# Windowed attention and a convolutional gated feed-forward: the order of TensorE, VectorE, ScalarE and GpSimd written in the source, with the weights' rescale moved to ScalarE

## The chip, the cores and the metric

The kernel runs on one core of one Trainium2 chip, all of it in float32. The metric is the device time of one launch in microseconds (us). The engines are TensorE (PE; its weight loads are PEld), VectorE (DVE), ScalarE (ACT), GpSimd (POOL) and SyncE (SP), which issues the DMA transfers.

## The reference

There are 8 batches of 576 tokens, 8 heads of 64, a window of 128 tokens, a model width of 512 and 1024 hidden channels. The weights are given in float64.

```
scores = q @ k^T / 8 + slope[h] * -|i - j|       # slope[h] = 2^-(h+1)
scores = where(0 <= i - j < 128, scores, -1e9)
attn   = exp(scores - rowmax);  attn /= rowsum + 1e-9
x      = (attn @ v)  as [B, S, H*D]              # 8 x 576 x 512
h      = relu(x @ w_in)                          # 512 -> 1024
conv   = sum over k of conv_w[k] * h[token + k - 1]   # 3 taps per channel, zero outside the batch
out    = (h * sigmoid(conv)) @ w_out             # 1024 -> 512
```

## The kernel before

**Tiles.** The 4608 tokens make 36 tiles of 128. A batch is 4.5 tiles long, so that some tiles begin a batch, some hold a border in their middle, and some follow such a tile. A query tile needs its own keys and those of the tile before; because the window is exactly 128, each place of a 128 x 128 score block is taken by one of the two, and VectorE merges them: a masked copy (`COPY_PREDICATED`, L261) puts the earlier tile's scores over the masked half, and a tile at a batch border has a second masked copy, with a large constant (its row ends in `_SCALAR`). The heads go in two halves, u = 0 and 1, of four.

**One tile through the kernel.** Names in brackets are those of the profile's rows.

- `qkT` transposes q and k on TensorE (pt) and ScalarE copies them out (L234, qkT_all).
- `scores`: matmuls (L254, sc); two merges, each a masked copy (L261) and the addition of the bias (L276, which writes e); the row maximum (L277, st); four exponentials on ScalarE, one for each head (L279); then sum, reciprocal and product on VectorE (L287 to L289), the normalisation.
- `attnT`: transposes on TensorE (pa), a copy by ScalarE (L299, rl), and one or two triangular masks on GpSimd (L302, L305), which part the merged block into the two key tiles.
- `av`: the context matmuls (L323, av). The context x is kept as a high part in the reduced type fp32r (L331, ScalarE) and a low part, the rest (L332, VectorE). `xfin` copies a halo column to the neighbouring chunk (L346, L348).
- The feed-forward works in 18 chunks of two tiles, with a halo column at either side, and in four steps a chunk, each over 256 of the 1024 channels: 72 steps. An **up** step has 24 matmuls (L368, p), three for each product, high by high, high by low, low by high. For either half: relu (L373, hh), the middle tap as a copy with a scale (L374, z), and two filter operations for the outer taps on VectorE (L381). A batch border within the chunk cuts these in pieces: four rows where two stand otherwise. Then tanh (L387), the gate's product (L388), and the split into high and low part (L393 on ScalarE, L394 on GpSimd; gh and gl). A **down** step multiplies that by the second weight (L409, o); after a chunk's last down step ScalarE copies the result out (L415, ob) and SyncE stores it.

**Weights.** They come as pairs of 32-bit words, in 17 blocks: four of the first weight, the small one of the convolution, four more of the first weight, eight of the second. A staging tile (wst, three buffers) takes each block. GpSimd clamps the high word read as a float (L133) and multiplies it by 2^-112 (L134, to wg); VectorE shifts the low word (L135) and joins the bits in two operations (L136, L139); ScalarE casts to the high part (L177); TensorE subtracts the two (L191, L192, pw), and ScalarE casts the rest to the low part (L193). A block's staging tile becomes free after L139, and the load of a later block goes into it.

**What sets the order.** `manual_schedule` holds TensorE alone to the order of the source. The other engines' lists are made by a scheduler, which runs a model of the timeline and weighs priorities that the source gives (150 for the context, 100 for the transposes, 60 for the scores, 15 for loads, 0 or -15 for the rest of the up steps, 600 for their matmuls). From tile 5 on the source's order is one loop, a period:

```
SC(t, 0); SC(t, 1); AV(t - 1); DOWN(); UP(); QK(t + 1)
TR(t, 0); UP(); TR(t, 1); DOWN()
```

Here `SC` is scores, `TR` is attnT and `AV` is av with xfin. Each period holds two up and two down steps. In odd t the first up step begins a new chunk, and its matmuls read a column that comes from the tile of this period's `AV(t - 1)`. In even t it begins a chunk's second half, whose x is long there. Ahead of the loop `opening` holds tiles 0 to 4, with the calls `WT(start, finish)` in between, which convert 14 of the 17 weight blocks; the other three stand in period 5. All transposes, scores, up steps and weights share six PSUM buffers (`pst`, tag "tr").

Of the kernel before, what the change touches and what calls it, by code (L numbers as in the profile page):

```python
# [21 lines left out]
def tile_alibi_window_attention_conv_glu(  # L22
# [102 lines left out]

    def to_f32(st, g):

        lo, hi = st[..., 0], st[..., 1]
# [1 line left out]
        nc.gpsimd.tensor_scalar(out=hf, in0=hf, scalar1=HIMAX, scalar2=-HIMAX, op0=ALU.min, op1=ALU.max)  # L133
        nc.gpsimd.tensor_scalar(out=gf, in0=hf, scalar1=2.0**-112, scalar2=None, op0=ALU.mult)  # L134
# [33 lines left out]
    started = []  # L168

    def convert_weight():  # L170
        block, st = fetched.pop(0)
        g = wpool.tile([P, WB], U32, name="wg", tag="wg")
        if block is None:
            f = to_f32(st, g[: 3 * NFC, :P])
        else:
# [1 line left out]
            nc.scalar.copy(out=block[1][0], in_=f)  # L177
# [49 lines left out]
    def qkT(t, u):  # L227
# [6 lines left out]
        nc.scalar.copy(out=qkT_all[:, t % SLOTS, u], in_=ps)  # L234

    def scores(t, u):
        first = (t * P) % S
        slot = t % SLOTS
# [16 lines left out]
        for a in range(2):  # L255
            ps = pss[a]
            s_cur, s_prev = ps[:, :, cur, :], ps[:, :, prev, :]
            shp = [P, 2, P]

            def put(mask, data):  # L260
                nc.vector.copy_predicated(  # L261
                    out=s_cur, mask=mask.unsqueeze(1).to_broadcast(shp), data=data
                )
# [329 lines left out]
```

## Time and profile before

| | |
|---|---|
| launches, median of 3 | 715.4 us (714.04 to 716.02) |
| the profiled execution | 713.98 us, of it 712.3 us in the span |
| TensorE busy, matmul | 656.5 us, 92% of the span, 4881 matmuls |
| TensorE busy, weight load (beside matmuls) | 561.7 us, 79% |
| VectorE busy | 516.9 us, 73% |
| ScalarE busy | 448.1 us, 63% |
| GpSimd busy | 236.2 us, 33% |
| mean granted TensorE clock | 0.973 of full speed |

The times in a row are in us from the start of the span, unless a column says ns. A row of the stretches by engine has: the stretch and its length; then busy time and count of PE, PEld, DVE, ACT and POOL; the granted clock; the share of the DMA engines; GB/s. A row of the waits has: the waiting instruction, what released it; the sum in us, how many times, and the longest or typical of one. A row of the timeline has: the start, the duration, engine, line, operation, output and inputs, shape, count, and in brackets the idle time of the engine ahead of it and what ended it. A row of the groups has: line, engine, operation, shape, count; busy us and mean ns; idle time ahead and its releasers.

### The profile page before, as it was taken

To read this page: it belongs to the slowest core of one execution; us is meant where nothing else is said; L and a number is where in the kernel's file an instruction comes from. 1 tells how busy PE (TensorE), PEld (TensorE's weight loads), DVE (VectorE), ACT (ScalarE), POOL (GpSimd) and SP (SyncE) were. 2 spreads that over 40 slices of the span, in tenths; PEclk is the share of its full clock that TensorE was granted. 3 is DMA by queue.
4 is the path that set the end of the run, shared out by engine and by line. 5 is a ranking of instruction groups with operands and counts; after the bars stand their busy time and mean duration, and the time that the engine had idled before them with its cause. 6 is when DMAs were issued, how large, how long until landed. Compare 5 with 4: busy or idle time off the path is not lost.

```text
span 712.3 us, 13254 instructions
## 1 busy us (share of the span) xinstructions
PE 656.5 (92%) x4881; PEld 561.7 (79%) x4881; DVE 516.9 (73%) x1208; ACT 448.1 (63%) x1257; POOL 236.2 (33%) x251
## 2 busy tenths in 40 slices
PE   5766897999999989999999998999999989999997
PEld 3445675888888878887978887888888878887996
DVE  7865997768776877777677677768776877777452
ACT  4544665767676746675767675767676746675563
POOL 3443861232223223333323333332223323333321
PEclk9967999999999999999999999999999999999999
DMA  9642440222221312222312222222222312200000
GB/s 229 149 129 58 124 128 16 75 45 75 61 60 45 80 40 75 45 75 45 90 31 75 45 75 45 76 46 75 60 60 46 81 38 75 46 31 1 31 31 30
DMA packets 120101, 47.02 MB, mean 66 GB/s; under 512 B 113356, under 2 KB 113380, under 8 KB 120036
## 3 DMA queue, kind: packets, MB, share of 16 engines
q1 hardware_dynamic: 120036, 46.17, 25.5%
q8 instruction: 39, 0.64, 0.4%
q14 instruction: 26, 0.21, 0.1%
HBM read 36.72 MB, written 9.44 MB: 65 GB/s over the span
## 4 chain that ended last, share of the span: by engine, by line
PE 63%; DVE 23%; ACT 8%; DMA 4%; issue 2%; POOL 1%; SPq 0%; ACTq 0%; POOLq 0%; DVEq 0%
PE p L368 29%; PE o L409 16%; DVE z L381 5%; PE sc L254 5%; PE av L323 4%; DVE sc L261 4%; PE pt L233 4%; DVE e L276 3%; PE pa L296 3%; DVE st L277 3%; DMA wst<-in_moe_w_out_dram 2%; ACT e L279 2%; DVE z L388 2%; ACT z L387 1%; DVE e L289 1%
## 5 line engine op out<-in xcount | busy, mean ns | idle before, releaser
L381 DVE SCALAR_TENSOR_TENSOR z<-hh,cw,z 128x256 f32<-128x256 f32 (+7 forms) x384 | 177.2, 493 | 104.9 <-ACT z L374 101.4
L368 PE MATMUL p<-x,wi 128*128 128x258 f32 x1728 | 228.5, 289 | 22.7 <-ACT e L279 8.8
L368 PEld LDWEIGHTS p<-x,wi 128*128 128x128 f32 x1728 | 219.2, 194 | 31.9 <-ACT e L279 14.9
L409 PE MATMUL o<-wo,gh 128*128 128x512 f32 x576 | 187.0, 405 | 0.7 <-ACT wo L193 0.7
L279 ACT ACTIVATE e<-e,st 128x128 f32<-128x128 f32 x288 | 112.2, 391 | 64.2 <-DVE st L277 63.8
L394 POOL TENSOR_TENSOR gl<-z,gh 128x512 fp32r<-128x512 f32 x72 | 94.6, 1314 | 132.8 <-ACT gh L393 124.5
L302 POOL TENSOR_SCALAR_AFFINE_SELECT rl<-rl 128x512 f32<-128x512 f32 x64 | 46.2, 721 | 266.1 <-ACT rl L299 266.1
L409 PEld LDWEIGHTS o<-wo,gh 128*128 128x128 f32 x576 | 103.0, 188 | 26.6 <-issue 5.8
L409 PE MATMUL o<-wo,gl 128*128 128x512 f32 x288 | 113.9, 396 | 0.0
L373 ACT ACTIVATE hh<-p 128x258 f32<-128x258 f32 x144 | 55.0, 382 | 70.5 <-PE p L368 68.6
L388 DVE SCALAR_TENSOR_TENSOR z<-z,hh 128x512 f32<-128x512 f32 x72 | 51.1, 709 | 52.7 <-ACT z L387 52.6
L323 PE MATMUL av<-rl,rv 128*64 128x128 f32 x1088 | 70.6, 282 | 13.0 <-POOL rl L305 13.0
L323 PEld LDWEIGHTS av<-rl,rv 128*64 128x64 f32 x1088 | 60.2, 140 | 25.9 <-POOL rl L305 15.0
L387 ACT ACTIVATE z<-z 128x512 f32<-128x512 f32 x72 | 45.3, 630 | 51.4 <-DVE z L381 49.5
L374 ACT ACTIVATE z<-hh,cw 128x256 f32<-128x256 f32 x144 | 73.8, 512 | 5.8 <-ACT hh L373 0.4
L254 PE MATMUL sc<-qkT_all 64*128 64x256 f32 x512 | 69.2, 410 | 6.0 <-ACT qkT_all L234 5.2
L254 PEld LDWEIGHTS sc<-qkT_all 64*128 64x128 f32 x512 | 49.0, 196 | 24.2 <-issue 10.9
L305 POOL TENSOR_SCALAR_AFFINE_SELECT rl<-rl 128x512 f32<-128x512 f32 x72 | 57.0, 792 | 30.0 <-ACT rl L299 26.0
L409 PEld LDWEIGHTS o<-wo,gl 128*128 128x128 f32 x288 | 54.1, 188 | 12.9
L393 ACT CAST gh<-z 128x512 fp32r<-128x512 f32 x72 | 44.4, 616 | 25.3 <-DVE z L388 25.2
L276 DVE SCALAR_TENSOR_TENSOR e<-sc,bias 128x256 f32<-128x256 f32 x144 | 54.3, 415 | 0.0
L279 ACT ACTIVATION_READ_ACCUMULATOR e<-e,st 128x1 f32 x288 | 53.9, 187 | 0.0
(64 smaller groups left out, 662.5 us busy)
## 6 DMA issues: line engine op xcount, KB each, us to landing
out_dram<-ob SPq DMA_DIRECT2D x36, 256.0 KB, 2.0
rqk<-in_q_dram SPq DMA_DIRECT2D x32, 256.0 KB, 3.1
rqk<-in_k_dram SPq DMA_DIRECT2D x32, 256.0 KB, 3.7
rv<-in_v_dram SPq DMA_DIRECT2D x32, 256.0 KB, 2.8
wst<-in_moe_w_in_dram SPq DMA_DIRECT2D x8, 512.0 KB, 4.7
wst<-in_moe_w_out_dram SPq DMA_DIRECT2D x8, 512.0 KB, 3.5
rqk<-in_q_dram SPq DMA_DIRECT2D x8, 128.0 KB, 2.8
rqk<-in_k_dram SPq DMA_DIRECT2D x8, 128.0 KB, 3.1
```

The source lines that it names most:

```text
L254: nc.tensor.matmul(pss[a][:, g], qt, qkT_all[rows, win, u, 1, g, :], start=True, stop=True)
L276: nc.vector.scalar_tensor_tensor(out=heads, in0=s_cur, scalar=-0.125, in1=b, op0=ALU.mult, op1=ALU.add)
L279: nc.scalar.activation(out=e[:, j, :], in_=e[:, j, :], func=AF.Exp, bias=st[:, 0, j : j + 1], scale=-1.0, accum_out=st[:, 1, j : j + 1],)
L305: nc.gpsimd.affine_select(out=r, in_=r, pattern=[[0, HU], [1, P]], compare_op=ALU.is_ge, fill=0.0, base=0, channel_multiplier=-1)
L323: nc.tensor.matmul(ps[a * D : (a + 1) * D, u * NG + g], vraw[tt][:, u * HU + j], rl[:, side, j], start=n == 0, stop=n == len(sides) - 1,)
L368: nc.tensor.matmul(ps[:, :XW], a[:, cc, f * P : (f + 1) * P], x[:, cc, :], start=n == 0, stop=n == last)
L373: nc.scalar.activation(out=hh[:, ff, :], in_=ps[:, :XW], func=AF.Relu, scale=0.5)
L374: nc.scalar.activation(out=z[:, ff, :], in_=hh[:, ff, 1 : 1 + CW], func=AF.Copy, scale=cw[:, 1, f : f + 1])
L381: nc.vector.scalar_tensor_tensor(out=z[:, ff, a:cut], in0=hh[:, ff, a + kk : cut + kk], scalar=cw[:, kk, f : f + 1], in1=z[:, ff, a:cut], ...
L388: nc.vector.scalar_tensor_tensor(out=z, in0=z, scalar=1.0, in1=hh[:, :, 1 : 1 + CW], op0=ALU.add, op1=ALU.mult)
L394: nc.gpsimd.tensor_tensor(out=gl, in0=z, in1=as32(gh), op=ALU.subtract)
L409: nc.tensor.matmul(oo[m], g[:, ff, ms], w[:, f, :], start=f == 0 and n == 0, stop=f == NFC - 1 and n == 2)
```

## The change

**One list an engine.** `manual_schedule` now holds TensorE, VectorE, ScalarE and GpSimd to the order of the source; SyncE alone is left to the scheduler, and the priorities are gone. For this, functions are cut into pieces that can be placed singly: `scores` into `scores` (matmuls), `merge` (one masked copy and its addition; L283, L296), `rowmax` (L300), `exps` (L305) and `normal` (L316 to L318); `qkT` into the transposes and `qkT_out` (L247); `av` into `av`, `x_hi` (L363) and `x_lo` with the halo (L367, L382); the up step into `up_half` (matmuls, relu, middle tap; L406 to L411), `conv` (L421), `gate` (tanh and product; L429, L430) and `split` (L438, L439). A step object carries one up step from piece to piece.

**Rescale on ScalarE.** The multiplication by 2^-112 is now an activation on ScalarE (L131); the clamp (L130) stays on GpSimd. The conversion has three parts: `begin_weight` (clamp and rescale), `convert_weight` (VectorE's three operations, ScalarE's high cast L186, and the fetch of the next block), and `finish_weight` (TensorE's subtraction, the low cast L203).

**Opening.** It now ends with tile 2; five blocks are converted in it. The other 12 stand in periods 3 to 5, by `w`: six, four and two. The initial loads come as q and k of tile 0, a block, q and k of tile 1, a block, v of tile 0, a block, v of tile 1; before, three blocks stood ahead of tile 1.

The core of the diff:

```diff
+    def rebias(st, g):
+        hf = st[..., 1].bitcast(F32)
+        nc.gpsimd.tensor_scalar(out=hf, in0=hf, scalar1=HIMAX, scalar2=-HIMAX, op0=ALU.min, op1=ALU.max)
+        nc.scalar.activation(out=g.bitcast(F32), in_=hf, func=AF.Copy, scale=2.0**-112)
...
-        nc.gpsimd.tensor_scalar(out=gf, in0=hf, scalar1=2.0**-112, scalar2=None, op0=ALU.mult)
...
+    def W(n=1):
+        for _ in range(n):
+            begin_weight()
+            if begun:
+                convert_weight()
+            if len(started) > 1:
+                finish_weight()
...
+        attnT(0, 0)
+        W()
...
+        attnT(1, 1)
+        W()
...
+        attnT(2, 1)
+        qk(3)
+        W(3)
+
+    def period(t, w=(0, 0, 0), first=True):
+        on = t < NT
+        late_split()
+        if on:
+            scores(t, 0)
+            scores(t, 1)
+            merge(t, 0, 0)
+            merge(t, 0, 1)
+            rowmax(t, 0)
+        av(t - 1)
+        loadv_ahead(t + 1)
+        if on:
+            exps(t, 0, range(0, 2))
+            merge(t, 1, 0)
+        x_hi(t - 1)
+        x_lo(t - 1)
+        if on:
+            exps(t, 0, range(2, HU))
+            merge(t, 1, 1)
+            rowmax(t, 1)
+        W_end()
+        if first:
+            down()
+        if on:
+            normal(t, 0)
+            exps(t, 1)
+        b = Step()
+        b.up()
+        b.half(0)
+        b.half(1)
+        if on:
+            normal(t, 1)
+        qk(t + 1)
+        b.conv()
+        W(w[0])
+        if on:
+            attnT(t, 0)
+        b.gate()
+        n = Step()
+        if not first:
+            b.split()
+            down()
+        n.up()
+        n.half(0)
+        if first:
+            b.split()
+        n.half(1)
+        n.conv()
+        W(w[1])
+        if on:
+            attnT(t, 1)
+        n.gate()
+        W(w[2])
+        gating.append(n)
...
+        down()
...
-    with tc.manual_schedule(engines={mybir.EngineType.PE}):
+    with tc.manual_schedule(engines={engines.PE, engines.DVE, engines.Activation, engines.Pool}):
         opening()
-        for t in range(5, NT + 1):
+        period(3, (2, 2, 2), first=False)
+        period(4, (1, 2, 1), first=False)
+        period(5, (2, 0, 0))
+        for t in range(6, NT + 1):
+            period(t)
+        tail()
```

TensorE's list is the same in both kernels from period 6 on. The other lists are not. VectorE's list at the start of period 15, an odd one, before (sc15 and e15 are this tile's scores and exponentials, the digit behind it is the half; av14 is the context of the tile before, x7 and x6 are chunks):

```order
L261 COPY_PREDICATED sc15_0_0_3129<-m_prev_88,sc15_0_0_3129 128x2x128
L261 COPY_PREDICATED sc15_0_1_3130<-m_prev_88,sc15_0_1_3130 128x2x128
L276 SCALAR_TENSOR_TENSOR e15_0_3127<-sc15_0_0_3129,bias_104 128x2x128
L276 SCALAR_TENSOR_TENSOR e15_0_3127<-sc15_0_1_3130,bias_104 128x2x128
L277 TENSOR_REDUCE st15_0_3128<-e15_0_3127 128x4
...
L277 TENSOR_REDUCE st15_1_3148<-e15_1_3147 128x4
L287 TENSOR_SCALAR st15_0_3128<-st15_0_3128 128x4
L288 RECIPROCAL st15_0_3128<-st15_0_3128 128x4
L289 TENSOR_TENSOR e15_0_3127<-e15_0_3127,st15_0_3128 128x512
L332 TENSOR_TENSOR x7_2980<-av14_3167,x7_2980 128x4x128
L346 CAST x6_2548<-x7_2980 128x8
```

The same place in the changed kernel:

```order
L283 COPY_PREDICATED sc15_0_0_3129<-m_prev_88,sc15_0_0_3129 128x2x128
L296 SCALAR_TENSOR_TENSOR e15_0_3127<-sc15_0_0_3129,bias_104 128x2x128
L283 COPY_PREDICATED sc15_0_1_3130<-m_prev_88,sc15_0_1_3130 128x2x128
L296 SCALAR_TENSOR_TENSOR e15_0_3127<-sc15_0_1_3130,bias_104 128x2x128
L300 TENSOR_REDUCE st15_0_3128<-e15_0_3127 128x4
L283 COPY_PREDICATED sc15_1_0_3137<-m_prev_88,sc15_1_0_3137 128x2x128
L296 SCALAR_TENSOR_TENSOR e15_1_3135<-sc15_1_0_3137,bias_104 128x2x128
L367 TENSOR_TENSOR x7_2966<-av14_3148,x7_2966 128x4x128
L382 CAST x6_2536<-x7_2966 128x8
...
L300 TENSOR_REDUCE st15_1_3136<-e15_1_3135 128x4
L316 TENSOR_SCALAR st15_0_3128<-st15_0_3128 128x4
```

The low part of x and the halo column move from behind the second half's maximum and the first half's normalisation to a place in the middle of the second half's merges, and each addition now stands right behind its own masked copy. ScalarE's list at the same place, before:

```order
L279 ACTIVATE e15_0_3127,st15_0_3128<-e15_0_3127,st15_0_3128 128x128 x4
L331 CAST x7_2980<-av14_3167 128x4x128
L279 ACTIVATE e15_1_3147,st15_1_3148<-e15_1_3147,st15_1_3148 128x128 x4
L373 ACTIVATE hh6_0_3201<-p6_0_3203 128x258
L374 ACTIVATE z6_0_3202<-hh6_0_3201,cw_117 128x256
```

And in the changed kernel:

```order
L305 ACTIVATE e15_0_3127,st15_0_3128<-e15_0_3127,st15_0_3128 128x128 x2
L363 CAST x7_2966<-av14_3148 128x4x128
L305 ACTIVATE e15_0_3127,st15_0_3128<-e15_0_3127,st15_0_3128 128x128 x2
L305 ACTIVATE e15_1_3135,st15_1_3136<-e15_1_3135,st15_1_3136 128x128 x4
L410 ACTIVATE hh6_0_3198<-p6_0_3200 128x258
L411 ACTIVATE z6_0_3199<-hh6_0_3198,cw_117 128x256
```

The high part of x moves ahead by two exponentials; relu follows the second half's exponentials in both. In the opening, ScalarE's list around the tanh of the first up step, before (hh0_0 and z0_0 belong to chunk 0's step 0; wi0 and wi1 are the high and low part of the first weight, wg a block under conversion, pw its subtraction):

```order
L374 ACTIVATE z0_0_548<-hh0_0_547,cw_117 128x256
L193 CAST wi1_114<-pw_598 128x512
L234 COPY qkT_all_118<-pt4_0_602 128x512
L387 ACTIVATE z0_0_548<-z0_0_548 128x512
L234 COPY qkT_all_118<-pt4_1_608 128x512
```

The same place in the changed kernel, in period 3:

```order
L411 ACTIVATE z0_0_539<-hh0_0_538,cw_117 128x256
L247 COPY qkT_all_118<-pt4_0_573 128x512
L247 COPY qkT_all_118<-pt4_1_578 128x512
L131 ACTIVATE wg_592<-wst_457 128x512
L186 CAST wi0_113<-wg_463 128x512
L131 ACTIVATE wg_601<-wst_469 128x512
L186 CAST wi0_113<-wg_592 128x512
L203 CAST wi1_114<-pw_610 128x512
L328 COPY rl3_0_619<-pa3_0_614 128x512
L429 ACTIVATE z0_0_539<-z0_0_539 128x512
```

Between the middle tap and tanh one weight cast stood there before; now two rescales, two high casts and a low cast stand there, and the copy for the transposed first half.

On GpSimd the clamp of a block stands behind the masks (L331, L334) that come ahead of it in the source, one or two a half tile; its rescale is gone, and so are the places of L134 between the masks.

More of the change, by code (lines that the diff above doesn't have):

```diff
@@ L153, in weight_blocks, with fetch_weight @@
             yield moe_w_out[f * P : (f + 1) * P, :], [w[:, f, :] for w in wo]
-    fetched = []
-    def fetch_weight(block):
+    fetched, begun, started = [], [], []
+    def fetch_weight():
+        if not blocks:
+            return
+        block = blocks.pop(0)
         st = wpool.tile([P, WB, 2], U32, name="wst", tag="wst")
@@ L233, in qkT, with qkT_out, window @@
                 nc.tensor.transpose(ps[:, i, g, :], rqk[:, i, h : h + 2, :].rearrange("p h d -> p (h d)"), ident)
-        nc.scalar.copy(out=qkT_all[:, t % SLOTS, u], in_=ps)
-    def scores(t, u):
+        pts[t, u] = ps
+    def qkT_out(t, u):
+        nc.scalar.copy(out=qkT_all[:, t % SLOTS, u], in_=pts.pop((t, u)))
+    def window(t):
         first = (t * P) % S
@@ L361, in up, with conv @@
+        def conv(fp):
+            hh, z = gs[fp]
             for ff in range(2):
                 f = 2 * fp + ff
[L363 to L371 removed]
@@ L459, in loads, with W_end, __init__, call @@
-    def loads(t):
+    def W_end():
+        while started:
+            finish_weight()
+    class Step:
+        def __init__(self):
+            self.on = bool(todo)
+            if self.on:
+                c, self.i = todo.pop(0)
+                if c not in fns:
+                    fns[c] = ffn_items(c)
+                self.fn = fns[c]
+        def call(self, k, *args):
+            if self.on:
+                self.fn[k](self.i, *args)
+        def up(self):
+            self.call(0)
+        def half(self, ff):
+            self.call(1, ff)
+        def conv(self):
+            self.call(2)
+        def gate(self):
+            self.call(3)
+        def split(self):
+            if self.on:
+                self.call(4)
+                downs.append(self)
@@ new lines, in qk, with soft @@
+            load_ahead(t + 2)
+    def soft(t, u):
+        merge(t, u, 0)
+        merge(t, u, 1)
+        rowmax(t, u)
+        exps(t, u)
+    def opening():
+        load(0)
+        fetch_weight()
+        load(1)
+        fetch_weight()
+        loadv(0)
+        fetch_weight()
+        loadv(1)
+        qk(0)
+        scores(0, 0)
+        scores(0, 1)
+        begin_weight()
+        soft(0, 0)
+        qk(1)
+        merge(0, 1, 0)
+        merge(0, 1, 1)
+        rowmax(0, 1)
+        scores(1, 0)
+        exps(0, 1)
+        normal(0, 0)
+        attnT(0, 0)
+        W()
+        normal(0, 1)
+        scores(1, 1)
+        attnT(0, 1)
+        soft(1, 0)
+        soft(1, 1)
+        normal(1, 0)
+        attnT(1, 0)
+        av(0)
+        x_hi(0)
+        loadv(2)
+        x_lo(0)
+        qk(2)
+        scores(2, 0)
+        normal(1, 1)
+        attnT(1, 1)
+        W()
+        scores(2, 1)
+        soft(2, 0)
+        av(1)
+        x_hi(1)
+        loadv(3)
+        soft(2, 1)
+        x_lo(1)
+        normal(2, 0)
+        attnT(2, 0)
+        normal(2, 1)
+        attnT(2, 1)
+        qk(3)
+        W(3)
@@ new lines, in tail @@
+    def tail():
+        late_split()
+        while todo:
+            b = Step()
+            b.up()
+            b.half(0)
+            b.half(1)
+            b.conv()
+            b.gate()
+            b.split()
+            down()
+        while downs:
+            down(0)
+    engines = mybir.EngineType
+    with tc.manual_schedule(engines={engines.PE, engines.DVE, engines.Activation, engines.Pool}):
+        opening()
+        period(3, (2, 2, 2), first=False)
[4 more added lines that the diff above has]
+        tail()
```

285 lines of the change are left out of this document (104 added, 181 removed).

## The prediction

> **What bounds the kernel now.** The page first: a span of 712.3 us in an execution of 713.98, so 1.7 us lie around it. TensorE is busy for 92% of it, but not evenly: the slices lose at the start.
>
> ```profile
> span 712.3 us, 13254 instructions
> PE   5766897999999989999999998999999989999997
> PEclk9967999999999999999999999999999999999999
> ```
>
> The stretches by engine say how much. A period (one token tile: scores, context, two downs, two ups) without a stall is the first row; the next three rows are periods 3 (from the first score of tile 3, at 49.90), 4 and 5, in which weights are still converted; the last is periods 6 and on.
>
> ```profile
> 311.02:328.15 17.13, 17.13 (x138) 15.13 (x137) 13.67 (x38) 11.84 (x34) 5.50 (x6) 1.00 0.29 78
> 49.90:77.06 27.16, 21.42 (x130) 16.82 (x131) 17.22 (x34) 13.97 (x38) 12.26 (x12) 0.77 0.41 105
> 77.06:105.80 28.74, 25.98 (x155) 19.16 (x154) 27.07 (x50) 16.90 (x45) 20.95 (x20) 0.94 0.43 125
> 105.80:132.56 26.76, 22.23 (x146) 17.88 (x145) 19.16 (x40) 15.76 (x41) 8.41 (x9) 0.94 0.14 31
> 132.56:680.00 547.44, 528.15 (x4130) 463.35 (x4130) 404.28 (x973) 362.51 (x1032) 165.61 (x176) 0.99 0.22 56
> ```
>
> TensorE fills a plain period to the last tenth, and from 132.56 to 680 only 547.44 - 528.15 = 19.3 us are idle. Periods 3 to 5 take 27.2 + 28.7 + 26.8 = 82.7 us, where three plain ones are 51.4. Who is waited for, from 132.5 on and then before it:
>
> ```profile
> PE p L368 <- ACT e L279: 8.8, 4, 2.8
> PE p L368 <- DVE st L287: 8.5, 9, 1.6
> PE p L368 <- DVE x L346: 1.9, 2, 1.0
> ...
> PE av L323 <- POOL rl L305: 13.0, 6, 4.5
> PE sc L254 <- ACT qkT_all L234: 5.2, 2, 3.3
> ```
>
> All late idle time is one wait, 15 times: the first up step of a chunk, in every odd period. The names of the releasers vary, the place doesn't. In the order of time (odd period 17, scores from 328.15):
>
> ```profile
> 330.44 0.75 DVE L261 COPY_PREDICATED sc<-m_prev,sc 128x256 f32<-128x256 uint8 x2
> 331.11 0.75 DVE L276 SCALAR_TENSOR_TENSOR e<-sc,bias 128x256 f32<-128x256 f32 x2
> 331.89 0.69 DVE L277 TENSOR_REDUCE st<-e 128x4 f32<-128x512 f32 x1
> 332.61 0.40 ACT L279 ACTIVATE e<-e,st 128x128 f32<-128x128 f32 x1 [1.43 <-DVE st L277]
> 334.17 0.57 ACT L331 CAST x<-av 128x512 fp32r<-128x512 f32 x1
> 335.55 0.68 DVE L332 TENSOR_TENSOR x<-av,x 128x512 fp32r<-128x512 f32 x1
> 336.27 0.17 DVE L346 CAST x<-x 128x8 fp32r<-128x8 f32 x1
> 336.59 3.12 PE L368 MATMUL p<-x,wi 128*128 128x258 f32 x24 [1.56 <-DVE st L287]
> 338.31 0.39 ACT L373 ACTIVATE hh<-p 128x258 f32<-128x258 f32 x1 [2.00 <-PE p L368]
> 342.25 0.63 ACT L387 ACTIVATE z<-z 128x512 f32<-128x512 f32 x1
> 345.78 1.51 DVE L381 SCALAR_TENSOR_TENSOR z<-hh,cw,z 128x256 f32<-128x256 f32 x2 [0.87 <-ACT z L374]
> 347.98 0.69 DVE L388 SCALAR_TENSOR_TENSOR z<-z,hh 128x512 f32<-128x512 f32 x1 [0.70 <-ACT z L387]
> ```
>
> The high part of x (L331) stands behind four exponentials, the low part (L332) behind a whole normalisation; the up step starts 6.15 us after the merges do (330.44 to 336.59).
>
> **Steady state: the wait shortens, the loop behind it does not.** From period 6 TensorE's order is unchanged; the other engines' order is what moves. New, x_hi follows two exponentials and x_lo one merge. From the start of the merges: merges 1.69, maximum 0.72 (331.89 to 332.61), two exponentials 0.78 (0.39 apart: four took 1.56 up to 334.17), x_hi 0.57 and 0.09 to be seen, x_lo 0.69, the halo column 0.17, 0.15 to TensorE: 4.86 instead of 6.15. The merges themselves were 1.45 (330.44 to 331.89). Now each masked copy is followed at once by the addition that reads it, where before two independent ones ran overlapped: 0.75 for two, 0.42 for one.
>
> ```profile
> L261 DVE COPY_PREDICATED sc<-m_prev,sc 128x256 f32<-128x256 uint8 x128 | 48.9, 421 | 1.5 <-PE sc L254 1.5
> ```
>
> So four in a chain are 2 x (0.45 + 0.42) less one overlap of 0.08, 1.66, with 0.03 to the next: 0.24 more. The Trainium skill ("VectorE: DVE Perf Modes", section on the DRAIN you can't avoid) says that an operation starts only when the pipeline is empty and that a semaphore between two costs nothing more; by it the new order of the merges would be free, and the time 717, the third rival below. The overlap of 0.08 in the row speaks for mine, and the page allows for it where nothing holds the next operation.
>
> The down step ahead of the up step ends 6.72 after the first score (317.74 in a plain period that began at 311.02), so the up step waits only if the merges start later than 6.72 - 4.86 = 1.85 into the period. Now they start at 1.5, or 2.3 after a period with a cut:
>
> ```profile
> 294.39 0.75 DVE L261 COPY_PREDICATED sc<-m_prev,sc 128x256 f32<-128x256 uint8 x2
> 326.83 2.25 DVE L381 SCALAR_TENSOR_TENSOR z<-hh,cw,z 128x192 f32<-128x192 f32 x4 [0.59 <-ACT z L374]
> 317.74 3.04 PE L368 MATMUL p<-x,wi 128*128 128x258 f32 x24
> ```
>
> (294.39 follows a first score at 292.88.) Were that kept, 15 of the 19.3 us would go. But ScalarE has the exponentials of the second half ahead of the up step's first relu, and these now come later, behind x_lo: 4.71 to the halo's end, merge and maximum 1.6, exponentials 1.66, so the relu starts 7.97 after the merges. Now it starts 7.87 after them (330.44 to 338.31), released by TensorE. What TensorE gains, ScalarE does not pass on. From the relu on I sum ScalarE's list by the spacing of the same operations here (0.41 to 0.53): 3.25 to tanh, 2.96 to the second filter pair, and from there to the next merges 2.8 as now (345.78, until 0.61 after 347.98): 9.0. The loop through VectorE and ScalarE is 17.0 us against TensorE's 17.13: it just fits in a plain period. A chunk with a batch border adds 0.95 (2.25 for 1.51, and 0.2 ahead of tanh; 12 of the 30 periods), a masked tile 1.3 (three rows like the next, two ahead of x_lo, one behind; 6 periods):
>
> ```profile
> 257.11 0.87 DVE L261 COPY_PREDICATED_SCALAR sc<-m_half,neg 128x256 f32 x2
> ```
>
> Now such an excess ends where the relu waits for TensorE again; in the new order the relu waits for ScalarE, so it is carried to the next period. Carried by hand through periods 6 to 35 (start 1.5, plus loop, less 17.13, less the stall; a tile that starts a batch saves TensorE 0.85), the stalls of the 15 odd periods are 0, 1.8, 0.6, 2.1, 1.4, 1.3, 1.6, 0, 1.6, 0.1, 2.2, 0.6, 2.1, 1.4, 1.3: 18 us, for 19.3. I take **-1**. Each 0.25 us of error in the loop moves that by 7, both ways: -8 to +7.
>
> **Opening: rescale on ScalarE, one list each.** A weight block costs now:
>
> ```profile
> L134 POOL TENSOR_SCALAR wg<-wst 128x512 f32<-128x512 f32 x16 | 26.2, 1638 | 12.0 <-PE pw L191 11.1 <-PE pcw L186 0.4
> L139 DVE SCALAR_TENSOR_TENSOR wg<-wst,wg 128x512 uint32<-128x512 uint32 x16 | 13.0, 813 | 0.2
> L177 ACT CAST wi<-wg 128x512 fp32r<-128x512 f32 x8 | 5.0, 620 | 11.6 <-DVE wg L139 11.6
> L193 ACT CAST wi<-pw 128x512 fp32r<-128x512 f32 x8 | 4.7, 584 | 3.4 <-PE pw L192 3.2
> 45.41 0.43 DVE L135 TENSOR_SCALAR wst<-wst 128x512 uint32<-128x512 uint32 x1 [0.86 <-DMA wst<-in_moe_w_in_dram]
> 46.82 0.68 DVE L136 SCALAR_TENSOR_TENSOR wg<-wg,wst 128x512 uint32<-128x512 uint32 x1
> 47.53 0.69 DVE L139 SCALAR_TENSOR_TENSOR wg<-wst,wg 128x512 uint32<-128x512 uint32 x1
> ```
>
> L134 leaves GpSimd (26.8 us with the small block), and ScalarE gets 17 operations like L177: 16 x 0.62, 10 us. VectorE does a block in 0.43 + 0.68 + 0.69 = 1.80 when undisturbed. ScalarE does 0.62 + 0.62 + 0.58 = 1.82.
>
> Up to the first score of tile 3 I take 47 us, 3 less than now: of the 13.0 us for GpSimd's masks half goes, and ScalarE's rescale gets a new wait instead, for the clamp (L133), which now stands behind two masks in GpSimd's list. The reordered loads put the same 1.5 MB ahead of tile 1's last: nothing.
>
> By then five of the 17 blocks are converted (now seven). The other 12 stand in periods 3 to 5, six, four and two, between a filter and its tanh, or behind a tanh. There ScalarE's list reads rescale, high cast, low cast, tanh: the cast waits for VectorE, tanh for the casts, VectorE's next step for tanh. So I count both engines' parts in series: 12 x 3.62 = 43.4, with 51.4 and two masked tiles 2.6: 97, less 1 for rescales that lie beside VectorE, 96. Period 6 begins at 47 + 96 = 143, not 132.6: **+10**. Bounds: if only VectorE's part counts, 51.4 + 21.6 + 2.6 = 76 and -10; if the staging buffer's refill is waited for too (the page gives 3.5 to 4.7 us to land) five more, +15. I take the series, since the lists leave nothing else for either engine to do there. The tail is a list of ups and downs as before: nothing. Sum: -1 + 10 = +9, 723 for 713.98; put on the median of the runs, 715.4, it is **724**. About 0.3%, 2 us, is what a measurement can tell.
>
> **Rivals.** *A, faster, 0.28:* the parts of a block overlap, as the scheduled order now gets them to in part (82.7 - 51.4 = 31 us for ten blocks, 3.1 each), so that VectorE's alone counts (-10), and the loop is 0.25 shorter (-7): 698. It decides where a block costs under 2.7 us. For it: GpSimd no longer slows VectorE (L139 0.81 mean, 0.69 alone). *B, slower still, 0.15:* the loop exceeds 17.25; then TensorE waits in every odd period, +7 and +10: 732. *C, no change, 0.12:* merges as cheap in the new order, loop 16.75, -8 and +10: 717. *Forecast, 0.45:* 724, itself 714 to 734. The cases give faster 0.30 (A and the forecast's edge), same 0.10, slower 0.60. The range from 702 to 736 leaves out half of A and the top of B.
>
> **What would show it.** First score of tile 6 at 143 (A: 122); of tile 3 at 47; in between ScalarE waiting for VectorE at the high cast and VectorE for tanh. Later: up steps 4.9 us after the merges, stalls of 18 us in all, unevenly spread and largest in masked tiles; relu without waits for TensorE. Stalls under 10, or a start of period 6 before 133, would make me wrong.

## The result and the profile after

The changed kernel takes 744.4 us (median of 4 runs, 742.86 to 748.98), 1.042 times the time of before [1.0375, 1.0472]. The profiled execution took 744.24 us with a span of 742.5, so 1.7 lie around it as before. Its stretches by engine, from the first scores of tiles 3, 4, 5, 6 and 35 on:

```profile
46.97:83.22 36.25, 22.65 (x129) 16.30 (x128) 24.74 (x47) 20.81 (x50) 9.20 (x11) 0.82 0.41 119
83.22:120.37 37.15, 27.70 (x152) 20.01 (x152) 22.73 (x44) 19.92 (x49) 10.20 (x12) 0.81 0.28 81
120.37:150.78 30.41, 23.73 (x143) 18.67 (x142) 19.48 (x38) 14.27 (x38) 4.65 (x6) 0.85 0.14 35
150.78:676.45 525.67, 500.53 (x3898) 439.15 (x3897) 424.17 (x928) 337.32 (x984) 151.88 (x166) 0.99 0.23 57
676.45:742.50 66.05, 58.77 (x401) 51.14 (x400) 35.84 (x65) 33.03 (x78) 16.76 (x16) 1.00 0.07 25
```

The same last two stretches of the kernel before:

```profile
132.56:648.57 516.01, 498.29 (x3897) 437.04 (x3896) 384.28 (x933) 344.68 (x986) 157.03 (x167) 0.99 0.23 58
648.57:712.30 63.73, 58.41 (x401) 51.25 (x400) 32.23 (x63) 33.30 (x76) 15.26 (x14) 0.99 0.07 26
```

| stage | before | after | difference |
|---|---|---|---|
| to the first score of tile 3 | 49.9 | 47.0 | -2.9 |
| periods 3 to 5 | 82.7 | 103.8 | +21.1 |
| periods 6 to 34 | 516.0 | 525.7 | +9.7 |
| rest | 63.7 | 66.1 | +2.3 |

The sum is +30.2, the difference of the spans. So the larger part of the loss lies in three periods of the opening, and the rest comes bit by bit. VectorE's busy time in periods 6 to 34 rose from 384 to 424 us with the same work: its operations have become longer, or ceased to overlap.

TensorE's late waits in these periods; then what relu waited for over the whole span in the kernel before, and relu's group now (its last two columns are idle time ahead of it and what ended that):

```profile
PE p L406 <- DVE x L382: 24.4, 12, 3.2
```
```profile
ACT hh L373 <- PE p L368: 68.6, 88, 5.8
```
```profile
L410 ACT ACTIVATE hh<-p 128x258 f32<-128x258 f32 x144 | 53.9, 374 | 6.7 <-PE p L406 6.5
```

The stall is at the same place as before, the chunk's first up step, but it grew; and relu, which before waited 68.6 us for TensorE, waits for it hardly at all. VectorE and ScalarE no longer follow TensorE: TensorE follows them. An odd period (its first score is at 348.97) in the order of time, VectorE:

```profile
353.19 0.42 DVE L283 COPY_PREDICATED sc<-m_prev,sc 128x256 f32<-128x256 uint8 x1
...
353.99 0.42 DVE L283 COPY_PREDICATED sc<-m_prev,sc 128x256 f32<-128x256 uint8 x1
354.45 0.42 DVE L296 SCALAR_TENSOR_TENSOR e<-sc,bias 128x256 f32<-128x256 f32 x1
354.91 0.69 DVE L300 TENSOR_REDUCE st<-e 128x4 f32<-128x512 f32 x1
...
362.17 1.92 DVE L421 SCALAR_TENSOR_TENSOR z<-hh,cw,z 128x256 f32<-128x256 f32 x4
...
365.69 3.68 DVE L421 SCALAR_TENSOR_TENSOR z<-hh,cw,z 128x256 f32<-128x256 f32 x4 [0.18 <-ACT z L411]
...
370.68 0.48 DVE L283 COPY_PREDICATED_SCALAR sc<-m_prev,neg 128x256 f32 x1
```

The up step's start, relu, tanh, and GpSimd's two gl in the same period:

```profile
358.06 0.48 PE L406 MATMUL p<-x,wi 128*128 128x258 f32 x2 [2.20 <-DVE x L382]
361.02 0.36 ACT L410 ACTIVATE hh<-p 128x258 f32<-128x258 f32 x1
364.13 0.65 ACT L429 ACTIVATE z<-z 128x512 f32<-128x512 f32 x1
354.01 1.29 POOL L439 TENSOR_TENSOR gl<-z,gh 128x512 fp32r<-128x512 f32 x1 [2.78 <-ACT gh L438]
366.25 1.29 POOL L439 TENSOR_TENSOR gl<-z,gh 128x512 fp32r<-128x512 f32 x1 [0.25 <-ACT gh L438]
```

The up step starts 4.87 us after the merges (353.19 to 358.06), relu 7.83 after them, tanh 3.11 after relu. But from merges to merges (353.19 to 370.68) it is 17.5 us, 0.4 more than TensorE needs. The four filter pieces of the first step took 1.92 us, those of the second 3.68: GpSimd's second gl runs beside these, with two masks behind it, and ScalarE's gh stands ahead of the second relu. The first gl runs beside merges, which keep their 0.42.

### The profile page after: what moved, and what is told of

Same layout as the page of the kernel before. It is cut to its first block, busy times and chain, and to the rows that moved or that the text cites. A ratio compares the mean times of both kernels' runs of the same rounds, so it can differ in the third digit from the quotient of the medians.

```text
span 742.5 us, 13277 instructions
## 1 busy us (share of the span) xinstructions
PE 663.2 (89%) x4881; PEld 565.6 (76%) x4881; DVE 559.9 (75%) x1208; ACT 451.7 (61%) x1274; POOL 205.0 (28%) x234
## 4 chain that ended last, share of the span: by engine, by line
DVE 52%; ACT 30%; PE 14%; issue 3%; POOL 1%; DMA 1%; ACTq 0%; SPq 0%; DVEq 0%; POOLq 0%
DVE z L421 19%; ACT e L305 11%; DVE sc L283 6%; DVE st L300 6%; DVE e L296 6%; PE p L406 5%; ACT z L429 5%; DVE z L430 5%; ACT z L411 4%; PE o L454 4%; DVE x L367 3%; ACT hh L410 2%; ACT x L363 2%; ACT qkT_all L247 2%; DVE e L318 2%
## 5 line engine op out<-in xcount | busy, mean ns | idle before, releaser
L406 PE MATMUL p<-x,wi 128*128 128x258 f32 x1728 | 230.3, 291 | 28.7 <-DVE x L382 28.6
L406 PEld LDWEIGHTS p<-x,wi 128*128 128x128 f32 x1728 | 220.7, 195 | 36.9 <-ACT e L305 31.9
L421 DVE SCALAR_TENSOR_TENSOR z<-hh,cw,z 128x256 f32<-128x256 f32 (+7 forms) x384 | 196.3, 554 | 28.0 <-ACT z L411 24.5
L305 ACT ACTIVATE e<-e,st 128x128 f32<-128x128 f32 x288 | 112.7, 393 | 132.5 <-DVE st L300 132.1
L439 POOL TENSOR_TENSOR gl<-z,gh 128x512 fp32r<-128x512 f32 x72 | 94.3, 1309 | 146.7 <-ACT gh L438 142.8
L331 POOL TENSOR_SCALAR_AFFINE_SELECT rl<-rl 128x512 f32<-128x512 f32 x64 | 43.4, 678 | 329.5 <-ACT rl L328 329.2
L430 DVE SCALAR_TENSOR_TENSOR z<-z,hh 128x512 f32<-128x512 f32 x72 | 54.7, 760 | 61.5 <-ACT z L429 61.5
L429 ACT ACTIVATE z<-z 128x512 f32<-128x512 f32 x72 | 45.8, 636 | 72.5 <-DVE z L421 72.5
L411 ACT ACTIVATE z<-hh,cw 128x256 f32<-128x256 f32 x144 | 73.5, 510 | 9.2 <-ACT hh L410 0.8
L352 PE MATMUL av<-rl,rv 128*64 128x128 f32 x1088 | 68.7, 278 | 0.7 <-POOL rl L334 0.6
L352 PEld LDWEIGHTS av<-rl,rv 128*64 128x64 f32 x1088 | 59.4, 138 | 12.8 <-issue 7.7
L334 POOL TENSOR_SCALAR_AFFINE_SELECT rl<-rl 128x512 f32<-128x512 f32 x72 | 54.6, 758 | 41.8 <-ACT rl L328 37.4
L296 DVE SCALAR_TENSOR_TENSOR e<-sc,bias 128x256 f32<-128x256 f32 x144 | 61.1, 425 | 4.9
L283 DVE COPY_PREDICATED sc<-m_prev,sc 128x256 f32<-128x256 uint8 x128 | 53.9, 421 | 14.1 <-PE sc L271 14.1
L438 ACT CAST gh<-z 128x512 fp32r<-128x512 f32 x72 | 44.5, 618 | 20.1 <-DVE z L430 20.1
```

The source lines that it names most:

```text
L283: nc.vector.copy_predicated(out=s_cur, mask=mask.unsqueeze(1).to_broadcast(shp), data=data)
L296: nc.vector.scalar_tensor_tensor(out=heads, in0=s_cur, scalar=-0.125, in1=b, op0=ALU.mult, op1=ALU.add)
L305: nc.scalar.activation(out=e[:, j, :], in_=e[:, j, :], func=AF.Exp, bias=st[:, 0, j : j + 1], scale=-1.0, accum_out=st[:, 1, j : j + 1],)
L352: nc.tensor.matmul(ps[a * D : (a + 1) * D, u * NG + g], vraw[tt][:, u * HU + j], rl[:, side, j], start=n == 0, stop=n == len(sides) - 1,)
L406: nc.tensor.matmul(ps[:, :XW], a[:, cc, f * P : (f + 1) * P], x[:, cc, :], start=n == 0, stop=n == last)
L411: nc.scalar.activation(out=z[:, ff, :], in_=hh[:, ff, 1 : 1 + CW], func=AF.Copy, scale=cw[:, 1, f : f + 1])
```

## Experiments on the steady state

Times are medians beside the kernel before on the same chip; the ratio is to before, with its interval. Where a kernel's own lists differ, its line numbers do too.

**s1: the split of a period's first step moved behind the second step's tanh.**

```diff
         n.half(0)
-        if first:
-            b.split()
         n.half(1)
...
         n.gate()
+        if first:
+            b.split()
         W(w[2])
```

> The changed kernel with one piece moved: the first step's split (gh on ScalarE, gl on GpSimd) stands behind the second step's tanh, no longer between its two relus. Theory GL (GpSimd's gl beside the second step's filters stretches them from 0.48 to 1.5 us, and the gh ahead of the second relu delays them): the loop from merges to merges falls from 17.48 us in a plain period to 16.1 to 16.8, the stalls at the chunk's first up step from 27 us to under 10, the time from 744 to 718-728. Rival LIST (the loop is long because the lists put VectorE and ScalarE in series, wherever the split stands): loop 17.4 or more, time 741-747.

Measured: 709.8 us, 0.9936 of before [0.9913, 0.9958], 34.6 us under the changed kernel. The same place as above in VectorE's list:

```profile
339.45 0.42 DVE L283 COPY_PREDICATED sc<-m_prev,sc 128x256 f32<-128x256 uint8 x1
...
351.94 2.27 DVE L421 SCALAR_TENSOR_TENSOR z<-hh,cw,z 128x256 f32<-128x256 f32 x4 [0.19 <-ACT z L411]
354.90 0.69 DVE L430 SCALAR_TENSOR_TENSOR z<-z,hh 128x512 f32<-128x512 f32 x1 [0.70 <-ACT z L429]
355.56 0.49 DVE L283 COPY_PREDICATED_SCALAR sc<-m_prev,neg 128x256 f32 x1
```

GpSimd's gl there, periods 6 to 34, and TensorE's wait in them:

```profile
355.46 1.28 POOL L439 TENSOR_TENSOR gl<-z,gh 128x512 fp32r<-128x512 f32 x1 [0.76 <-ACT gh L438]
```
```profile
150.00:644.89 494.89, 493.11 (x3898) 434.77 (x3897) 394.10 (x932) 336.46 (x984) 150.28 (x167) 1.00 0.24 61
```
```profile
PE p L406 <- DVE x L382: 1.8, 3, 0.7
```

The filter pieces take 2.27 instead of 3.68, the loop 16.11 instead of 17.49; gl now starts when the gate's product is nearly done, and lies beside the merges, which take 0.42 to 0.49. The stall is gone, 24.4 to 1.8 us, and these periods fell by 31 us. (The masks still lie beside the second step's filters: 2.27, not 1.92.) Theory GL holds: the loop is at the low end of its range, and the time 8 us under the 718 to 728 that it gave. The edit moves two things, gl on GpSimd and gh on ScalarE.

**s2: gl left out.** The low part of the gate's product isn't computed; a tile of zeros is multiplied in its place.

```diff
-            gl = fpool.tile([P, 2, CW], F32R, name=f"gl{c}_{fp}", tag="gl", bufs=3)
+            gl = gl_zero
             nc.scalar.copy(out=gh, in_=z)
-            nc.gpsimd.tensor_tensor(out=gl, in0=z, in1=as32(gh), op=ALU.subtract)
```

> The changed kernel without gl: the low part of the gate's product is left out, a constant tile of zeros is multiplied in its place, so TensorE does the same work and GpSimd only has masks and clamps; ScalarE's gh stays where it is. Theory GL: third filter piece 0.75 us earlier, loop 16.7 to 16.9 in a plain period, 17.6 with a cut, time 726-734. Rival LIST: loop 17.4 or more, time 741-747.

Measured: 718.7 us, 1.0053 [1.0035, 1.0071]. From merges to merges, with the second pair of the second step's filters between, and periods 6 to 34:

```profile
342.62 0.42 DVE L285 COPY_PREDICATED sc<-m_prev,sc 128x256 f32<-128x256 uint8 x1
...
356.41 1.42 DVE L423 SCALAR_TENSOR_TENSOR z<-hh,cw,z 128x256 f32<-128x256 f32 x2 [0.22 <-ACT z L413]
...
359.13 0.48 DVE L285 COPY_PREDICATED_SCALAR sc<-m_prev,neg 128x256 f32 x1
```
```profile
148.06:652.56 504.50, 496.25 (x3897) 437.38 (x3896) 397.15 (x929) 339.11 (x985) 75.67 (x108) 0.99 0.24 60
```

The loop is 16.51, the periods 21.2 us shorter than in the changed kernel; the time came out 7 us under the range that GL gave. Of s1's 31 us gl is therefore about 21. The other 10 I put down to gh's place: it stays here between the relus, and the second pair still waits for the scaled copy behind it (L413). No run moves gh alone.

**s4: gl alone moved, nothing left out.** gh stays between the relus; gl goes behind the second half's masks and the second tanh (pieces 6 and 7 of a step are gh and gl).

```diff
-            b.split()
+            b.call(6)
         n.half(1)
...
         n.gate()
+        if first and b.on:
+            b.call(7)
+            downs.append(b)
```

> The changed kernel with gl alone moved: the first step's gh stays between the second step's two relus on ScalarE, its gl on GpSimd stands behind the masks of the second half and the second step's tanh. Nothing is left out. Theory PLACE (what costs is GpSimd's gl beside the filters, 21 us of the steady state as without gl): loop 16.5 in a plain period, time 721-726. Rival SHADOW (gl at its new place slows other VectorE work, the gate's product, the merges, the normalisation, as much): loop 17.2 or more, time 735-745. The distance from s1 (709.8) is then what gh ahead of the second relu costs.

Measured: 740.2 us, 1.0369 [1.0335, 1.0403]. I expected 721 to 726; the rival SHADOW holds. VectorE from merges to merges, and GpSimd's gl:

```profile
350.10 0.42 DVE L283 COPY_PREDICATED sc<-m_prev,sc 128x256 f32<-128x256 uint8 x1
...
366.03 1.60 DVE L430 SCALAR_TENSOR_TENSOR z<-z,hh 128x512 f32<-128x512 f32 x1 [0.70 <-ACT z L429]
367.55 0.48 DVE L283 COPY_PREDICATED_SCALAR sc<-m_prev,neg 128x256 f32 x1
```
```profile
365.81 1.27 POOL L447 TENSOR_TENSOR gl<-z,gh 128x512 fp32r<-128x512 f32 x1
```

gl left the filters and hit the gate's product: 1.60 instead of 0.69, and the loop is 17.45 again. In s1 gh stands behind the second tanh, so gl starts 0.56 after the gate's product (355.46 against 354.90), not 0.22 ahead of it.

**m1: the first half's merges in the old order**, two masked copies, then two additions.

```diff
-            merge(t, 0, 0)
-            merge(t, 0, 1)
+            masked(t, 0, 0)
+            masked(t, 0, 1)
+            added(t, 0, 0)
+            added(t, 0, 1)
```

> The changed kernel with the first half's merges in the order of before in every period: two masked copies, then two additions. Theory DEPEND (an addition right behind the masked copy that it reads costs 0.13 us each, 0.27 a half): merges to maximum 1.45 instead of 1.72 us, loop 17.2 instead of 17.48, stalls 5 to 8 us fewer, time 736-740. Rival FREE (the order of independent and dependent operations costs nothing): merges to maximum 1.7, time 742-747.

Measured: 735.2 us, 1.0281 [1.0256, 1.0306]. VectorE's merges to the maximum, and periods 6 to 34:

```profile
350.05 0.75 DVE L287 COPY_PREDICATED sc<-m_prev,sc 128x256 f32<-128x256 uint8 x2
350.71 0.74 DVE L305 SCALAR_TENSOR_TENSOR e<-sc,bias 128x256 f32<-128x256 f32 x2
351.49 0.69 DVE L309 TENSOR_REDUCE st<-e 128x4 f32<-128x512 f32 x1
```
```profile
151.26:668.90 517.64, 499.68 (x3897) 438.88 (x3896) 418.49 (x928) 337.63 (x984) 152.06 (x166) 0.99 0.23 57
```

1.44 instead of 1.72 from the first merge to the maximum, and the periods are 8.0 us shorter: DEPEND holds, with a time just under its range.

## Experiments on the opening and on the parts

**o1: TensorE's subtraction later**, behind the transposes of the same half and behind the next tile's scores.

```diff
-        W(w[1])
         if on:
             attnT(t, 1)
+        W(w[1])
         n.gate()
-        W(w[2])
+        W(w[2], finish=False)
...
-        if not blocks:
+        if t == 5:
             W_end()
```

(W(w[0]) likewise.) All of a place's weight work moves with the subtraction: GpSimd's clamps now stand behind the masks, ScalarE's rescales and casts behind the copy of the transposes.

> The changed kernel with TensorE's subtraction of the weights (pw) placed behind the transposes of the exponentials and behind the next tile's scores in periods 3 to 5. Theory PW (each time the subtraction waits for VectorE's block and then holds back transposes, tanh or scores: 9.0% of the chain of the 103.8 us): first score of tile 6 at 139-143 instead of 150.8, time 733-737. Rival SERIES (VectorE's and ScalarE's shares of the blocks alone fill the 104 us, TensorE's waits are slack): first score of tile 6 at 148-152, time 742-747.

Measured: 739.4 us, 1.0342 [1.0307, 1.0378]; periods 3 to 5:

```profile
48.25:146.83 98.58, 73.71 (x423) 55.92 (x422) 69.75 (x129) 54.70 (x136) 25.99 (x28) 0.84 0.30 83
```

5.2 us less than 103.8, half of what PW gave; tile 6 at 146.8 lies between both ranges. What the subtraction does in the changed kernel is plain, though, in TensorE's waits in these periods and in the chain of waits (start, duration):

```profile
PE pw L201 <- DVE wg L141: 25.4, 6, 6.7
```
```profile
72.66 2.04 PE pw L201 x2
...
75.13 0.87 PE pa L325 x4
...
80.79 2.07 PE pw L201 x2
...
83.29 2.06 PE sc L271 x8
```

TensorE comes to the subtraction, waits there for VectorE's block (six times, 25.4 us), and only then does the transposes that ScalarE copies ahead of tanh, or the next scores. In o1 16.9 us of that wait are left.

**o2: rescale back on GpSimd.**

```diff
-        nc.scalar.activation(out=g.bitcast(F32), in_=hf, func=AF.Copy, scale=2.0**-112)
+        nc.gpsimd.tensor_scalar(out=g.bitcast(F32), in0=hf, scalar1=2.0**-112, scalar2=None, op0=ALU.mult)
```

> The changed kernel with the rescale back on GpSimd, all else as it is. Theory SERIES (each block costs ScalarE's rescale of 0.62 on the chain): 12 x 0.62 = 7 us less, time 736-739. Rival (the rescale is off the chain, since it runs beside VectorE's first operation, and GpSimd's 1.64 us slow VectorE instead): time 744-752.

Measured: 745.6 us, 1.0433 [1.0396, 1.0471], within a us or so of the changed kernel; periods 3 to 5 take 105.9 us for 103.8. SERIES falls. By itself the run could also mean that GpSimd's rescale costs as much as ScalarE's; but in the changed kernel's chain of waits through these periods no rescale (L131) appears. It isn't on the path there.

**x2: the kernel before with the rescale on ScalarE, and nothing else.**

```diff
-        nc.gpsimd.tensor_scalar(out=gf, in0=hf, scalar1=2.0**-112, scalar2=None, op0=ALU.mult)
+        nc.scalar.activation(out=gf, in_=hf, func=AF.Copy, scale=2.0**-112)
```

> The kernel before with the rescale on ScalarE, nothing else. Theory OFF (in a scheduled opening the rescale lies beside other work on either engine): 712-717. Rival SERIES (17 x 0.62 on ScalarE's path): 720-726. Rival GAIN (GpSimd's 26.8 us of rescales were on the path): 705-711.

Measured: 705.9 us, 0.9869 [0.9813, 0.9924]. The rescale's group, and periods 3 to 5:

```profile
L134 ACT ACTIVATE wg<-wst 128x512 f32<-128x512 f32 (+1 forms) x17 | 10.8, 650 | 1.3 <-POOL wst L133 1.1
```
```profile
48.08:124.93 76.85, 65.36 (x429) 50.48 (x429) 62.55 (x125) 51.79 (x133) 26.66 (x30) 0.93 0.33 91
```

GAIN holds: a rescale takes 0.65 us for 1.64, it almost never waits, and periods 3 to 5 take 76.9 instead of 82.7; the time to their end fell by 7.6 us of the 9 (124.93 for 132.56).

**x1: the changed kernel with TensorE alone in the source's order.**

```diff
-    with tc.manual_schedule(engines={engines.PE, engines.DVE, engines.Activation, engines.Pool}):
+    with tc.manual_schedule(engines={engines.PE}):
```

> The changed kernel with only TensorE held to the source's order, as before: the cut code, the new TensorE order and ScalarE's rescale stay, and the scheduler makes VectorE's, ScalarE's and GpSimd's lists without the old priorities. Theory LISTS (the loss lies in the written lists of the three engines): 705-725. Rival CODE (TensorE's new opening order and the rescale on ScalarE bring most of the loss by themselves): 735 or more.

Measured: 710.8 us, 0.9924 [0.9894, 0.9954]; periods 3 to 5 (periods 6 to 34 take 516.8 us, as before):

```profile
47.66:128.93 81.27, 66.50 (x423) 52.71 (x422) 62.13 (x127) 53.43 (x135) 24.55 (x27) 0.89 0.33 94
```

LISTS holds: cut code, ScalarE's rescale and TensorE's new opening order together are 4 us faster than before; the three written lists cost the other 34.

**o3: the high cast one place later**, where the next block is begun, so that ScalarE doesn't wait there for VectorE's part of the same block.

```diff
-        if block is not None:
-            nc.scalar.copy(out=block[1][0], in_=f)
-        started.append((block, f))
+        joined.append((block, f))
...
+    def cast_weight(keep):
+        while len(joined) > keep:
+            block, f = joined.pop(0)
+            if block is not None:
+                nc.scalar.copy(out=block[1][0], in_=f)
+            started.append((block, f))
```

(In periods 3 to 5 `W` holds one block back in this way.)

> The changed kernel with the weights' high cast one place later in periods 3 to 5: a block is cast where the next one is begun, so ScalarE need not wait for VectorE's part of the same block ahead of tanh. Theory SERIES (ScalarE waits 11 us for VectorE at the casts, VectorE then 13 us for tanh; in series): first score of tile 6 at 142-146 instead of 150.8, time 736-740. Rival BOUND (VectorE's work and TensorE's subtraction set the time of these periods, the casts' waits lie beside): first score of tile 6 at 149-152, time 742-747.

Measured: 733.9 us, 1.0267 [1.0239, 1.0294], better than SERIES gave:

```profile
46.91:137.88 90.97, 71.33 (x422) 51.20 (x422) 68.22 (x129) 53.80 (x136) 24.05 (x28) 0.87 0.32 92
```

91.0 for 103.8 us. The two engines were in series at the cast.

**c1: s1, o1 and o3 together.** The edits are those above.

> All four lists written out, with three of the moves together: the first step's split behind the second step's tanh (s1), the subtraction behind transposes and scores (o1), the high cast one place later (o3). Theory ADD (casts 13 us and subtraction 4 us are separate waits of the opening): first score of tile 6 at 132-135, time 691-696. Rival SAME (both take away the same wait): first score of tile 6 at 137-139, time 697-700.

Measured: 702.1 us, 0.9808 [0.9754, 0.9863]; neither range. Periods 3 to 5, and ScalarE's longest wait in them:

```profile
47.44:142.60 95.16, 72.80 (x423) 52.59 (x422) 67.62 (x129) 53.49 (x136) 25.66 (x28) 0.86 0.31 89
```
```profile
ACT wg L131 <- POOL wst L130: 14.7, 7, 3.0
```

In these periods it is worse than o3 alone. A wait that took 5.3 us in o3 became ScalarE's longest: the rescale now waits 14.7 us for GpSimd's clamp, which came behind the masks when the weights' place moved behind the transposes.

**c2: as c1, the clamps ahead of the masks.**

```diff
         n.conv()
+        clamp_weight(w[1])
         if on:
             attnT(t, 1)
         W(w[1], keep=1)
```

> As c1, with GpSimd's clamp of the blocks placed ahead of the masks of the same place in periods 3 to 5, no longer behind them. Theory CLAMP (in c1 the waits taken away come back as ScalarE's wait for a clamp that stands behind the masks, some 5 to 8 us in periods 4 and 5): first score of tile 6 at 134-138, time 693-698. Rival LOADS (the staging loads, and a TensorE at a low clock, hold periods 4 and 5 back): first score of tile 6 at 141-144, time 700-704.

Measured: 698.2 us, 0.9763 [0.9739, 0.9788], just short of the range; tile 6 at 136.9:

```profile
47.24:136.89 89.65, 69.53 (x422) 51.75 (x421) 67.64 (x129) 53.39 (x136) 24.47 (x28) 0.90 0.32 91
```

The clamp was 5.5 us of c1's shortfall. What is left beside x2's 76.9 isn't settled: the rescale still waits 6.6 us for a buffer that TensorE's subtraction holds.

**h1: the opening of before, s1's steady state.** Up to tile 5 only TensorE's order is written, with the source of before (rescale on GpSimd), then all four.

```diff
+    with tc.manual_schedule(engines={engines.PE}):
...
+        opening()
...
     with tc.manual_schedule(engines={engines.PE, engines.DVE, engines.Activation, engines.Pool}):
-        opening()
-        period(3, (2, 2, 2), first=False)
-        period(4, (1, 2, 1), first=False)
-        period(5, (2, 0, 0))
         for t in range(6, NT + 1):
             period(t)
```

> The first step's split behind the second step's tanh, as in s1, and the opening of the kernel before: up to tile 5 TensorE's order alone is written out, the other engines' lists are the scheduler's, rescale on GpSimd; from tile 6 on all four lists are written out. Theory PARTS (the opening's loss of 17.4 us against before, first score of tile 6 at 150.0 instead of 132.6, and the steady state's gain of 21 us are independent): first score of tile 6 at 131-134, time 709.8 - 17.4 = 692 (690-695). Rival CARRY (the scheduled opening leaves VectorE or ScalarE behind, and the steady state pays it back): first score of tile 6 as before, but time above 698.

Measured: 692.5 us, 0.9691 [0.967, 0.9713]. PARTS holds. Tile 6 starts at 134.6, half a us past its range and 2 us later than before, and the periods are those of s1:

```profile
134.57:629.65 495.08, 493.39 (x3898) 434.83 (x3897) 394.93 (x934) 337.07 (x985) 150.11 (x167) 1.00 0.24 61
```

**h2: h1 with m1's merges.** The edit is that of m1.

> As h1 (opening of before, first step's split late), with the first half's merges as two masked copies and then two additions, the edit that brought 9 us in m1. Theory TENSORE (the loop now fits within TensorE's 17.13 us and only 1.7 us of stalls are left): 690.5-693. Rival LOOP (VectorE's and ScalarE's loop still sets the time): 683-688.

Measured: 690.2 us, 0.9648 [0.9596, 0.9701], just below TENSORE's range and 2 us above LOOP's. The edit that brought 9 us where the loop was the bound brings about 2 where TensorE is, and the intervals of h1 and h2 overlap.

**h3: h2 with the rescale on ScalarE.** The edit is that of x2, in the scheduled opening.

> As h2 (scheduled opening of before, four written lists from tile 6 on), with the rescale on ScalarE. Theory ADD (the rescale's gain is made in the opening, the steady state's apart from it): first score of tile 6 at 125-128, time 690.2 less 8 = 682 (680-685). Rival NOT (the scheduler's lists for the cut code give it no such gain): 688-692.

Measured: 681.2 us, 0.9525 [0.9502, 0.9548], the fastest of all, 33 us under before. Periods 3 to 5 take 78.1 us; periods 6 to 34:

```profile
125.11:618.00 492.89, 492.71 (x3897) 434.97 (x3897) 389.82 (x934) 339.69 (x986) 153.18 (x167) 1.00 0.25 61
```

In 492.89 us TensorE is idle for 0.2. The parts add up: the list edits of the steady state and the rescale in the opening are apart from each other.

## Why the prediction was wrong

The forecast was slower, 724 us, 702 to 736; it came out slower, at 744.4, outside the range. The sign of the whole was right, and that of the opening; the steady state, forecast at a small gain, is a loss.

**The steady state, forecast at -1 (-8 to +7): +9.7 to tile 35, +2.3 behind it.** The early steps of the loop held to 0.15 us: the up step 4.87 us after the merges (4.86 forecast), relu at 7.83 (7.97), tanh 3.11 later (3.25). The step that failed is "2.96 to the second filter pair, and from there to the next merges 2.8 as now". Measured it is 6.55 (364.13 to 370.68), 0.8 more, and nearly all of that lies ahead of the second pair. I followed ScalarE's list to the scaled copy that the second pair needs; that copy ended at 366.99, as forecast. But VectorE was still at the first pair, which took 1.11 in the kernel before, and 2.13 here, where gl (366.25 to 367.54) runs beside it:

```profile
343.80 1.11 DVE L381 SCALAR_TENSOR_TENSOR z<-hh,cw,z 128x256 f32<-128x256 f32 x2 [0.19 <-ACT z L374]
```
```profile
365.69 2.13 DVE L421 SCALAR_TENSOR_TENSOR z<-hh,cw,z 128x256 f32<-128x256 f32 x2 [0.18 <-ACT z L411]
366.48 0.51 ACT L411 ACTIVATE z<-hh,cw 128x256 f32<-128x256 f32 x1
```

The second pair came 0.7 later than forecast for it; the 1.51 that I took for this pair was near (about 1.6). So the sum put GpSimd at nothing: it never asked where gl lies in the new list, and gl stands there right on the second step's filters. In s2, without gl, the second pair starts 2.88 after tanh and the next merges 2.72 after that, a little under the forecast's 2.96 and 2.8. The loop is 17.5, not 17.0, and rival B's condition (over 17.25) is met; its price of +7 would have been near. s1, s2 and s4 show the cause: the split away from filters and gate, 31 us; gl alone gone, 21; gl moved onto the gate, 4 by the medians.

The Trainium skill ("SBUF — State Buffer", section Who interferes with whom) says that a VectorE instruction with two inputs in SBUF contends with a GpSimd instruction that reads SBUF, and one with at most one such input, outside the modes that use two ports, doesn't. The rows agree: filters and the gate's product, which read z and hh, are stretched (0.69 to 1.60); masked copies and additions, whose scores lie in PSUM, are not (0.42 to 0.49 beside gl).

**The merges' order, "0.24 more".** Right: 0.28 by m1, 8 us over these periods. The third rival, merges as cheap in the new order, falls: an addition starts 0.46 after the masked copy of 0.42 that it reads (353.99 to 354.45), and two independent copies of 0.42 each took 0.75 together. By the rule of the Trainium skill ("VectorE: DVE Perf Modes", section The DRAIN you can't avoid) that a semaphore between two operations costs nothing extra the new order would be free; here it costs 0.28.

**The opening, forecast at +10 (-10 to +15): +18.2.** Tile 3's first score came at 47, as forecast (46.97), but largely by luck: of TensorE's 13.0 us of waits for masks only 4.1 lay ahead of tile 3. These went, and TensorE waits there now 4.8 and 3.7 us for the normalisation, which the forecast didn't have.

Periods 3 to 5 took 103.8 us, not 96. That "the cast waits for VectorE, tanh for the casts, VectorE's next step for tanh" was right in part, and o3 gets 12.8 us from it. But the step that failed is the sum "12 x 3.62 = 43.4, with 51.4 and two masked tiles 2.6". In the chain of waits through each of these periods, added up, the blocks stand with about 29 us, not 43: VectorE's operations with 15.6, ScalarE's casts with 2.2 and its rescale with nothing, where 21.8 were counted for ScalarE, and TensorE's subtraction (L201, L202) with 11.4, where nothing was counted. All else on the chain has about 74 us, where the sum took 54 from undisturbed periods. So 96 came near only because the two errors go against each other. x2 shows the rescale as a gain of 9.

TensorE's subtraction waits for VectorE's block and holds back transposes and scores. The clock granted to TensorE was 0.81 and 0.85 in periods 4 and 5, for 0.94 before, and right behind these waits it was 0.50:

```profile
83.29:85.35 2.06, 2.06 (x11) 1.72 (x12) 0.02 (x1) 1.14 (x3) 0.83 (x1) 0.50 0.75 264
```

Eight score matmuls take 2.06 us there; at a granted clock of 1.00 sixteen take 1.93 (132.63 in the kernel before). The clock was 0.50 too from 72.66 to 76.00, 80.79 to 82.87, 108.41 to 111.00 and 136.01 to 139.34; the kernel before has such a place as well (83.55 to 85.85). An estimate: the four subtractions at these places and what TensorE does right behind them, 14.6 us of the chain, would take about half at the full clock. "From period 6 on TensorE's order is unchanged" was true, and I looked no further at its order ahead of that. How the rest divides stays open: o1 moved the weight work and gained 5 us, and no run changes the clock or the subtraction alone.

**Rival A**, that the parts of a block overlap, is near what the scheduler makes of these parts: 81.3 us for periods 3 to 5 in x1, 76.9 in x2, where A had 76.

## What to carry to other kernels

Before an engine's order is written out by hand, walk the list of every engine that shares something with the one you mean to relieve: here a GpSimd operation that hardly anything waits for cost 21 us at the place where it ran (s2), and moved to another bad place it cost nearly as much (s4). Then ask of each edit which loop bounds the kernel at that place: 0.28 us a period were worth 9 us where VectorE's and ScalarE's loop was the bound, and about 2 where TensorE was. In this kernel written lists paid in the regular loop, once gl had its place (495 us for 516 in periods 6 to 34); the irregular opening was done better by the scheduler, and both can stand in one kernel.

## What was not expected of the hardware

- In s4 a GpSimd subtraction of 128 x 512 held a VectorE operation that reads two SBUF tiles nearly to its own end: the gate's product, 0.69 us when alone, began at 366.03 within gl (365.81 to 367.08) and ended at 367.63. GpSimd itself lost little: gl takes 1.27 to 1.30 in the rows shown, and at most 1.48 in the changed kernel.
- The same multiplication by a constant, 128 x 512, takes 0.65 us on ScalarE (x2) and 1.64 on GpSimd (the kernel before), both means.
